# A three-stage kernel on one core: tiles of the expert items padded to one residue modulo 512 bytes, small products in fewer groups, and a reordered first item

## The chip, the cores and the metric

The kernel runs on one core of one Trainium2 chip. The metric is the device time of one execution in microseconds (us), as the median of several runs. Times inside an execution come from the profile of one execution; they count from its first instruction. Engines: PE is TensorE (PEld its weight loads), DVE is VectorE, ACT is ScalarE, POOL is GpSimd, SP is SyncE, which issues nearly all DMAs here.

## The reference

Three stages follow one another: an attention between 512 tokens and 32 states per head and batch, a mixture of 8 experts with top-1 routing and a skip, and a dense feed-forward layer.

```python
# attention: x (8,8,512,64), state (8,8,32,64) -> (8,8,544,64), both directions of a softmax
# regrouped to 4352 tokens of 512
skip_score = x @ w_skip                  # only tokens with a score over 0 are computed
logits = xc @ w_gate; e = argmax(logits) # expert of each token, gate = its softmax probability
h = np.maximum(xc[mask] @ w1[e], 0.0)    # 512 -> 1024
y[mask] = gate_w[mask, None] * (h @ w2[e])
out[do_compute] = xc + y
# dense layer, 512 -> 2048 -> 512
h = x @ w_in
g = h * np.clip(h + 3.0, 0.0, 6.0) / 6.0
return g @ w_out
```

## The kernel before

The order of the work on every engine is the order in which the program issues it; each engine runs its own queue in that order, and so does SP with the DMAs.

The attention routes each token and scatters its row to a buffer `xs` in HBM, sorted by expert. The expert stage (class `Experts`) then works through items. A large item is 512 rows of one expert: `run` does the first in `first()` and four more in `item_a(i, conv)`, i = 1 to 4. A large item has eight slices f of the hidden width. `s1a(f)` makes 12 products of 128x128 by 128x512 from `w1p` and `xTa` (L849), then a Relu on ACT (L853) and a remainder on DVE (L854) into `hT`; `s2a(po, f)` makes 12 products from `hT` and `w2p` (L861). The program issues `s1a(f)`, then `s2a(po, f - 1)`. Each operand is kept as a rounded part and a remainder, so a fetched weight slice is cut by `split1`, `split2` (ACT L761, DVE L762) before use. `end_a` ends an item: it turns the next item's rows (`turn`, L768: four transposes and a split) between the last products, gates the result on DVE (L891) and scatters it to `x_in` by four indirect DMAs on POOL (L725).

A small item is 64 rows of one expert, in plain float32 (`item_b`, a generator). In a large item i the program steps through small item i - 1: ten steps, one at f = 0 and nine at the places in `SMALL_AT`, where entry 2f is behind `s1a(f)` and 2f + 1 behind `s2a(f - 1)`. Four steps are first-layer products (L1053, 4 records each), one turns the hidden rows (L1003), four are second-layer products (L1069, 8 records each). Its weights come as eight chunks of 512 KB through three rooms; a chunk's room is refilled by SP (L1026) when the products that read it are done. Further small items, if there are any, run in a loop (`For_i`, L1112) behind the last large item.

Beside the items the kernel converts the dense layer's weights (`convert`, a generator `conv` stepped in `item_a`; fetched by `W.load`, L1219 and L1223; DVE steps L1240 to L1262) and stores them. In `first()` the list `some(n)` works through the last batch's routing (`rest`: L428, L408, L414, then counts L342, the plan of the items, the scatters) and one converted slice, stored by SP at L1306 and L1307. The second half of the plan, `second()`, is called as `k["tables"]`: three PE transposes (L652), then four DVE operations (L656 to L659) that fill `lim`, `tab_b` and `nb`.

SP's fetches for item 1 in `first()` start at f = 3: first the 512 rows (`fetchx`, L715, 1028 KB), then weight slices in pairs (`fetch1` L704, `fetch2` L710, 512 KB each), at f = 6 the small item's rows (L1016 to L1018) and three chunks (L1026).

The tiles lie one after another in each partition. The pool `a_x` holds, in this order, `raw1` twice (8192 bytes each), three `XR` slots (8480 bytes, 16·512 + 288), three `X` slots (8224 bytes, 16·512 + 32), `srows` (4112 bytes, 8·512 + 16) and `XT` (8192). `xTa` lies in `X` slots, `hT` in an `XR` slot. Behind it come small tiles and then `w1p` and `w2p` (16384 bytes a part). The dense layer (L1440, L1460, L1542, L1594) has tiles of its own whose sizes are multiples of 512 bytes; they begin below `a_x`, where its pools are closed by then.

Of the kernel before, what the change touches and what calls it, by code (L numbers as in the profile page):

```python
# [9 lines left out]
F32 = mybir.dt.float32  # L10
# [11 lines left out]
P = 128  # L22
# [4 lines left out]
XW = DM + 2  # L27

# [22 lines left out]
def attention(tc, ctx, pools, x, state, w_skip, w_gate, x_in, xs, slot, acc, count, k, consts, fill, side, early):  # L51
# [16 lines left out]
    def load(b):  # L68
        t = xp.tile([P, 4 * XW], F32, tag="X", name="X")[:, 0:4 * DM]
# [27 lines left out]
    st = xp.tile([P, 4 * 2 * NB], F32, tag="XR", name="st")[:, 0:2 * B * D].rearrange("p (g d) -> p g d", d=D)  # L97
# [294 lines left out]
    srows = xp.tile([P, 2, XW], F32, name="srows", bufs=1)  # L392
# [137 lines left out]
    def rest(plan):  # L530
# [9 lines left out]
        yield lambda: r2(b)  # L540
        pt = turned()
# [9 lines left out]
        yield lambda: r6(b)  # L551
# [38 lines left out]
Q = 64  # L590
ROUND = 1.5 * 2.0 ** 23


def plan(tc, sp, c, early, k):
# [50 lines left out]
    def second():  # L645

        pt = k["turned"]()
        vals = [red[:, 4:5], red[:, 1:2], red[:, 3:4]]
        lim, tb = k["lim"], k["tab_b"]

        def turn(i):
            nc.tensor.transpose(pt[:, i, :], vals[i].to_broadcast([P, P]), k["ident"])  # L652

        return [
            lambda: [turn(i) for i in range(3)],
            lambda: v.tensor_copy(lim, pt[:, 0, 0:NSMALL]),  # L656
            lambda: v.tensor_scalar(tb[:, 0, :], pt[0:1, 1, 0:NSMALL], 7.0, None, op0=ALU.min),
            lambda: v.tensor_scalar(tb[:, 1, :], pt[0:1, 2, 0:NSMALL], float(NSLOT), None, op0=ALU.min),
            lambda: v.tensor_scalar(k["nb"], eb[0:1, 8:9], float(NA), None, op0=ALU.max),  # L659
        ]  # L660
# [4 lines left out]
class Experts:  # L665
# [7 lines left out]
    def __init__(self, tc, pools, w1, w2, xs, x_in, k, W):  # L673
# [4 lines left out]
        self.tab_e = self.sp.tile([1, 2], I32, name="tab_e", bufs=1)  # L678
        self.room1 = [self.xp.tile([P, 4, DM], F32, name=f"raw1_{i}", bufs=1) for i in range(2)]
# [39 lines left out]
    def rows(self, name, tag="XR"):  # L719

        t = self.xp.tile([P, 4 * XW if tag == "X" else 4 * DM + 72], F32, tag=tag, name=name)
# [24 lines left out]
    def room(self):  # L746
        for i in range(2):
            t = self.xp.tile([P, 4 * XW], F32, tag="X", name=f"xTa{i}")
            self.xTa.append(t[:, 0:4 * DM].bitcast(F32R).rearrange("p (k c) -> p k c", k=4))

    def load2(self, i):
        t = self.xp.tile([P, 4 * DM + 72 * i], F32, tag="XR" if i else "XT", name="raw2", bufs=3 if i else 1)
# [21 lines left out]
    def run(self, ctx, c2, tail, plan, after):  # L774
# [30 lines left out]
        self.hT = self.xp.tile([P, 4 * DM + 72], F32, tag="XR", name="hT")  # L805
# [3 lines left out]
        keep_p = ctx.enter_context(tc.tile_pool(name="m_k", bufs=1))  # L809
        ca = ExitStack()  # L810
# [3 lines left out]
        xb = [keep_p.tile([P, DM // 2 + 2], F32, name=f"xb{i}") for i in range(2)]  # L814
        seen = keep_p.tile([P, 1], F32, name="seen")
        toks = keep_p.tile([P, 10], I32, name="toks")
        drops = keep_p.tile([P, 2], F32, name="drops")
        t = self.hT
        hT = [t[:, 4 * DM // 2 * i:4 * DM // 2 * (i + 1)].bitcast(F32R).rearrange("p (f c) -> p f c", f=NF) for i in range(2)]
        xTb = self.xp.tile([P, 2, XW], F32, tag="srows", name="xTb", bufs=1)  # L820
# [23 lines left out]
        def s1a(f):  # L844
            ph = p_h.tile([P, 512], F32, tag="h", name="ph")
            n = 0
            for kk in range(4):
                for a, b in PAIRS:
# [3 lines left out]
                    n += 1  # L852
            nc.scalar.activation(hp[f][0], ph, AF.Relu)  # L853
# [45 lines left out]

        def convert():  # L900

            todo = list(range(NEARLY, NFF))
            raw = {todo[0]: self.W.load(todo[0])}
            for i, f in enumerate(todo):
                parts, steps = self.W.cut(raw.pop(f))
                for n, step in enumerate(steps):
                    step()
                    if n == 4 and i + 1 < len(todo):
# [5 lines left out]
        def first():  # L914

            split1(0)
            split1(1)
            some(8)
            po = accs()
            for f in range(NF):  # L920
                split2(f)
                s1a(f)
# [3 lines left out]
                if f + 2 < NF:  # L926
                    split1(f + 2)
                if f == 3:
# [884 lines left out]
```

## Time and profile before

| | |
|---|---|
| runs | 1165.72, 1162.03, 1165.53 us; median 1165.53 us |
| profiled execution, its own time | 1166.02 us |
| its span, first to last instruction | 1164.3 us |
| mean granted TensorE clock | 0.985 |
| PE busy | 1112.9 us, 96% of the span |
| DVE, ACT, POOL busy | 72%, 41%, 10% |

The profile gives busy times per engine, the span in slices, the DMA queues, the chain of work that ended last, and groups of instructions by source line. The trace behind it answers questions on any stretch. A row of a timeline is start, duration, engine, line, operation, tiles, shapes and count; in brackets stands the idle time of the engine before it and what ended it. Neighbouring equal instructions are merged into one row, and matmuls overlap in part, so the time per matmul is read from the starts of consecutive runs.

### The profile page before, as it was taken

The page shows a single profiled execution, that of the slowest core. Times are in us where ns is not written, and L with a number is a line of the kernel's source. Part 1 is how long each engine was busy: PE and PEld are TensorE (multiplying, and loading weights), DVE is VectorE, ACT ScalarE, POOL GpSimd, SP SyncE. Part 2 cuts the span into 40 slices and gives each one's busy share as a digit, 9 for nine tenths or more (in the row PEclk, how much of TensorE's full clock was granted, in tenths as well). Part 3 has the DMA queues.
Part 4 walks back from the last instruction along what each step waited for, and adds up shares of the span by engine and source line. Part 5 has one row for each costly group of instructions (what it writes and reads, how often), then busy time and mean ns, then how long its engine had stood idle before and what let it go on. Part 6 is the DMA issues. An engine that isn't in the chain of part 4 may idle for free.

```text
span 1164.3 us, 16315 instructions
## 1 busy us (share of the span) xinstructions
PE 1112.9 (96%) x5978; PEld 920.0 (79%) x5978; DVE 834.1 (72%) x1632; ACT 482.0 (41%) x922; POOL 114.8 (10%) x170
## 2 busy tenths in 40 slices
PE   7887898999999949999999999999999999999998
PEld 4555676776766738888899998899989999899997
DVE  5978565766667736676788767786888678876776
ACT  6885342433333314545333244334333343334331
POOL 5466121020202020000000000000000000000000
PEclk9999898999999979999999999999999999999999
DMA  7985676987886677964552365425551454334432
GB/s 200 290 280 200 210 260 214 340 282 282 287 281 227 233 229 277 377 251 181 199 207 101 118 217 184 152 86 197 206 205 49 181 205 156 128 118 175 187 136 91
DMA packets 89074, 238.56 MB, mean 205 GB/s; under 512 B 13440, under 2 KB 40576, under 8 KB 83488
## 3 DMA queue, kind: packets, MB, share of 16 engines
q1 hardware_dynamic: 84480, 226.33, 55.2%
q0 software_dynamic: 4512, 11.17, 2.6%
q8 instruction: 48, 0.79, 0.3%
q14 instruction: 34, 0.28, 0.1%
HBM read 177.80 MB, written 63.22 MB: 207 GB/s over the span
## 4 chain that ended last, share of the span: by engine, by line
PE 61%; DVE 1%; ACT 0%; issue 0%; ACTq 0%
PE o L1594 28%; PE b L1542 24%; PE o L1460 4%; PE b L1440 4%; PE o L1371 1%; ACT g L1268 0%; PE b L1371 0%; DVE cv L1385 0%; DVE g L1269 0%; DVE c L1556 0%; DVE xt L1269 0%; DVE cv L1556 0%; DVE gg L1385 0%; ACT gg L1384 0%; DVE wc L1269 0%
## 5 line engine op out<-in xcount | busy, mean ns | idle before, releaser
L1594 PE MATMUL o<-wo,g 128*128 128x512 f32 x1440 | 334.3, 390 | 0.0
L1594 PEld LDWEIGHTS o<-wo,g 128*128 128x128 f32 x1440 | 269.7, 188 | 54.7
L1542 PE MATMUL b<-xc,wc 128*128 128x384 f32 x1680 | 299.6, 335 | 1.6 <-ACT c L1566 1.6
L1542 PEld LDWEIGHTS b<-xc,wc 128*128 128x128 f32 x1680 | 292.2, 188 | 4.0 <-ACT c L1566 1.9
L1269 DVE TENSOR_TENSOR g<-cv,g 128x384 fp32r<-128x384 f32 x160 | 89.4, 558 | 92.8 <-ACT g L1268 92.8
L1268 ACT CAST g<-cv 128x384 fp32r<-128x384 f32 x160 | 82.2, 514 | 156.9 <-DVE cv L1385 156.9
L861 PE MATMUL po<-w2p,hT 128*128 128x512 f32 x480 | 124.2, 407 | 2.3 <-ACT hT L853 2.3
L849 PE MATMUL ph<-xTa,w1p 128*128 128x512 f32 x480 | 122.8, 407 | 0.0
L861 PEld LDWEIGHTS po<-w2p,hT 128*128 128x128 f32 x480 | 90.3, 192 | 31.0 <-ACT hT L853 6.7
L849 PEld LDWEIGHTS ph<-xTa,w1p 128*128 128x128 f32 x480 | 89.8, 191 | 29.6 <-issue 9.6
L1384 ACT ACTIVATE cv<-cv,three 128x384 f32<-128x384 f32 x80 | 49.2, 615 | 143.5 <-DVE cv L1556 136.0
L1556 DVE TENSOR_TENSOR c<-b,c 128x384 f32<-128x384 f32 x160 | 87.3, 552 | 16.7 <-PE b L1542 16.2
L1603 DVE SCALAR_TENSOR_TENSOR hl<-o,hl 128x512 f32<-128x512 f32 x140 | 92.8, 683 | 2.1 <-PE o L1594 2.0
L854 DVE SCALAR_TENSOR_TENSOR hT<-ph,hT 128x512 fp32r<-128x512 f32 x40 | 27.6, 690 | 51.0 <-ACT hT L853 48.7
L853 ACT ACTIVATE hT<-ph 128x512 fp32r<-128x512 f32 x40 | 23.9, 596 | 82.5 <-PE ph L849 76.6
L1384 ACT ACTIVATE cv<-c,three 128x384 f32<-128x384 f32 x80 | 49.2, 615 | 15.0 <-DVE g L1269 15.0
L1556 DVE TENSOR_TENSOR cv<-b,cv 128x384 f32<-128x384 f32 x80 | 44.4, 555 | 14.2 <-PE b L1542 12.8
L1385 DVE SCALAR_TENSOR_TENSOR cv<-cv,c 128x384 f32<-128x384 f32 x80 | 44.2, 552 | 5.8 <-ACT cv L1384 4.8
L279 PE MATMUL pxr<-BD,AT 128*128 128x265 f32 x128 | 40.3, 435 | 8.0 <-ACT XR L283 3.4
L1603 DVE SCALAR_TENSOR_TENSOR acc<-o,acc 128x512 f32<-128x512 f32 x70 | 44.9, 683 | 1.3 <-PE o L1594 1.3
L1385 DVE SCALAR_TENSOR_TENSOR cv<-cv,cv 128x384 f32<-128x384 f32 x80 | 44.0, 550 | 0.0
L1250 ACT ACTIVATE raw<-raw 128x512 f32<-128x512 f32 x32 | 22.0, 689 | 51.5 <-DVE cv L1246 48.8
(287 smaller groups left out, 1270.1 us busy)
## 6 DMA issues: line engine op xcount, KB each, us to landing
wc<-wc SPq DMA_DIRECT2D x36, 1792.0 KB
wo<-wo SPq DMA_DIRECT2D x37, 1024.0 KB
raw<-in_moe_w_dram SPq DMA_DIRECT2D x40, 512.0 KB
spare<-in_moe_w_dram SPq DMA_DIRECT2D x32, 512.0 KB
raw<-in_moe_w_in_dram SPq DMA_DIRECT2D x16, 512.0 KB
raw<-in_moe_w_out_dram SPq DMA_DIRECT2D x16, 512.0 KB
x_in_dram<-XR SPq DMA_DIRECT2D x8, 1024.0 KB
wo<-hl SPq DMA_DIRECT2D x16, 512.0 KB
```

Of the source, the lines that this page charges most:

```text
L849: nc.tensor.matmul(ph, lhsT=w1p[a][:, f, kk, :], rhs=xTa[b][:, kk, :], start=(n == 0), stop=(n == 11))
L861: nc.tensor.matmul(po[c], lhsT=hp[f][a][:, P * c:P * c + P], rhs=w2p[b][:, f, :], start=(f == 0 and n == 0), stop=(f == NF - 1 and n == 2),)
L1268: nc.scalar.copy(hi, src)
L1269: nc.vector.tensor_tensor(lo, src, hi.bitcast(F32), op=ALU.subtract)
L1384: nc.scalar.activation(gg, h, AF.Relu, bias=k["three"])
L1385: nc.vector.scalar_tensor_tensor(gg, gg, 6.0, h, op0=ALU.min, op1=ALU.mult)
L1440: nc.tensor.matmul(ph, lhsT=w1(f, a, kk), rhs=xt[b][:, kk, :], start=(n == 0), stop=(n == 11))
L1460: nc.tensor.matmul(pos[c], lhsT=gg[a][:, P * c:P * c + P], rhs=w2(f, b), start=(f == 0 and n == 0), stop=(f == NFF - 1 and n == 2),)
L1542: nc.tensor.matmul(t, lhsT=w[:, s:s + P], rhs=XC[m // NP][:, x, b, kk, :], start=(i == 0), stop=(i == 5))
L1556: v.tensor_tensor(c, t, u, op=ALU.add)
L1594: nc.tensor.matmul(po, lhsT=gs[f][a][:, o:o + P], rhs=w[:, DM * (2 * f + b):DM * (2 * f + b) + DM], start=(q == 0), stop=(q == 5),)
L1603: nc.vector.scalar_tensor_tensor(dst, po, 1.0 / 6.0, dst, op0=ALU.mult, op1=ALU.add)
```

## The change

- Sizes. All `X` and `XR` slots become `ROWS` = 4·(512 + 32) floats, 8704 bytes, 17·512. `srows` becomes 4608 bytes. A pad of 72 floats is put ahead of `raw1`, one of 80 floats ahead of `w1p`.
- Small products. `SMALL_AT` puts them in four groups instead of eight in items 1 to 3. In item 4 (`SMALL_LAST`) the four first-layer products are in two groups and the four second-layer products come behind `end_a`; its chunks have more rooms.
- First item. `product(f + 1)` is issued ahead of `relu(f)`, `product(0)` ahead of the routing's rest; `split1(f + 2)` moves ahead of `relu`. SP fetches weights first and the 512 rows at f = 5, the chunks ahead of the small item's rows, and the first slice for `conv` at f = 7. `r6` moves ahead of the counts. `tables` is cut: one transpose and `lim` behind `end_a`, the rest in item 1 at f = 4; the load of `nb` into the engines' registers moves to item 4. `convert` fetches its next slice at its step 0 instead of 4.

```diff
+ROWS = 4 * (DM + 32)
-        t = xp.tile([P, 4 * XW], F32, tag="X", name="X")[:, 0:4 * DM]
+        t = xp.tile([P, ROWS], F32, tag="X", name="X")[:, 0:4 * DM]
-            XR[b] = xp.tile([P, 4, 2 * NB], F32, tag="XR", name="XR")
+            XR[b] = xp.tile([P, 4, ROWS // 4], F32, tag="XR", name="XR")[:, :, 0:2 * NB]
+        self.xp.tile([P, 72], F32, name="pad", bufs=1)
         self.room1 = [self.xp.tile([P, 4, DM], F32, name=f"raw1_{i}", bufs=1) for i in range(2)]
-        self.hT = self.xp.tile([P, 4 * DM + 72], F32, tag="XR", name="hT")
+        self.hT = self.xp.tile([P, ROWS], F32, tag="XR", name="hT")
+        keep_p.tile([P, PAD], F32, name="pad2")
         def first():
             split1(0)
+            ph = product(0)
             split1(1)
-            some(8)
+            split2(0)
+            some(9)
             po = accs()
             for f in range(NF):
-                split2(f)
-                s1a(f)
+                if f:
+                    split2(f)
+                now = ph
+                if f + 1 < NF:
+                    ph = product(f + 1)
+                if f + 2 < NF:
+                    split1(f + 2)
+                relu(f, now)
                 some((16, 16, 12, 10, 8, 10, 16, 12)[f])
-                if f + 2 < NF:
-                    split1(f + 2)
                 if f == 3:
-                    self.fetchx(row_a(0), xn[1])
-                    for g in range(0, 6, 2):
-                        self.fetch1(e0, g)
-                    for g in range(0, 4, 2):
-                        self.fetch2(e0, g)
+                    self.fetch1(e0, 0)
+                    self.fetch1(e0, 2)
+                    self.fetch2(e0, 0)
+                    self.fetch1(e0, 4)
+                    self.fetch2(e0, 2)
                 if f == 5:
                     self.fetch1(e0, 6)
                 if f in (5, 7):
                     self.fetch2(e0, f - 1)
+                if f == 5:
+                    self.fetchx(row_a(0), xn[1])
                 if f == 6:
-                    fetch_b(row_b(0), xb[0])
                     b0 = expert_b(0)
                     for c in range(3):
                         fetch_w(b0, c, chunks[c])
+                    fetch_b(row_b(0), xb[0])
+                if f == 7:
+                    next(conv)
             some(999)
-            for step in k["tables"]():
-                step()
             end_a(po, 0, False)
             split1(6)
             split1(7)
+            for step in tables()[:2]:
+                step()
         def item_a(i, conv):
-            small = item_b(i - 1, chunks, h32, xb[0], x32[0], hs, yb[0], 0, 1 if more else 0)
+            small = item_b(i - 1, chunks if more else chunks + free1 + chunks[:1], h32, xb[0], x32[0], hs, yb[0], 0, 1 if more else 0)
+                if f == 4 and i == 1:
+                    for step in tables()[2:]:
+                        step()
             end_a(po, i, not more)
+            for _ in small:
+                pass
-SMALL_AT = (2, 4, 5, 7, 9, 11, 12, 13, 14)
+SMALL_AT = (3, 3, 6, 6, 8, 10, 10, 14, 14)
+SMALL_LAST = (3, 3, 6, 6, 8)
```

## Rows read from the trace of the kernel before

**Rows 1.** The page's chain that ended last, shares of the span by engine.
```profile
PE 61%; DVE 1%; ACT 0%; issue 0%; ACTq 0%
```

**Rows 2.** Busy time by stage: start:end, length, engines (count), clock, DMA share, GB/s.
```profile
172.84:184.76 11.92, 9.56 (x46) 7.77 (x45) 6.54 (x15) 4.90 (x9) 0.19 (x1) 0.86 0.90 310
184.76:246.07 61.31, 58.79 (x265) 41.41 (x264) 38.04 (x66) 22.11 (x40) 6.83 (x10) 0.97 0.77 272
246.07:303.41 57.34, 57.08 (x265) 40.38 (x264) 37.51 (x65) 22.21 (x40) 7.48 (x10) 1.00 0.81 283
360.75:415.92 55.17, 55.17 (x247) 38.49 (x245) 42.13 (x72) 20.66 (x37) 8.83 (x13) 1.00 0.65 220
415.92:430.12 14.20, 0.00 (x1) 0.03 (x1) 4.75 (x10) 1.04 (x1) 3.60 (x5) 0.62 0.62 213
430.12:1164.30 734.18, 727.33 (x3640) 648.87 (x3640) 541.04 (x1009) 280.84 (x516) 0.00 (x0) 1.00 0.48 176
```

**Rows 3.** Timeline of PE in the first large item.
```profile
147.64 2.97 PE L849 MATMUL ph<-xTa,w1p 128*128 128x512 f32 x12
150.44 2.96 PE L861 MATMUL po<-w2p,hT 128*128 128x512 f32 x12
```

**Rows 4.** The chain of work in the dense layer: start, duration, what.
```profile
446.61 2.72 PE b L1440 x12
449.33 2.72 PE o L1460 x12
```

**Rows 5.** Timeline of PE in large item 2.
```profile
252.88 3.06 PE L861 MATMUL po<-w2p,hT 128*128 128x512 f32 x12
255.78 2.95 PE L849 MATMUL ph<-xTa,w1p 128*128 128x512 f32 x12
258.66 1.08 PE L1053 MATMUL phb<-spare,xTb 128*64 128x512 f32 x4
259.67 2.60 PE L861 MATMUL po<-w2p,hT 128*128 128x512 f32 x10
```

**Rows 6.** Waits of PE, 120 to 445 us: total, times, longest.
```profile
PE prl L414 <- issue: 3.0, 1, 3.0
PE ptx L768 <- DVE toks L869: 2.4, 1, 2.4
PE po L861 <- ACT hT L853: 2.3, 1, 2.3
```

**Rows 7.** Busy time of two short stretches, columns as in rows 2.
```profile
129.30:136.10 6.80, 6.62 (x21) 5.13 (x22) 2.37 (x11) 0.88 (x3) 0.75 (x2) 0.50 0.50 172
201.00:204.40 3.40, 3.40 (x9) 2.49 (x9) 2.80 (x6) 1.24 (x3) 0.00 (x0) 0.50 0.64 212
```

**Rows 8.** Timeline of DVE at the start of the first large item.
```profile
126.40 1.29 DVE L762 TENSOR_TENSOR w1p<-raw,w1p 128x512 fp32r<-128x512 f32 x2 [0.57 <-issue]
```

**Rows 9.** Timeline of PE at the start of the first large item.
```profile
130.79 5.46 PE L849 MATMUL ph<-xTa,w1p 128*128 128x512 f32 x12
```

**Rows 10.** Timeline of SP in the first large item.
```profile
158.36 0.35 SPq L715 DMA_DIRECT2D xr<-xs_dram  x1
...
164.99 1.26 SPq L710 DMA_DIRECT2D raw<-in_moe_w_dram  x1
```

**Rows 11.** Busy time of 159 to 173 us, columns as in rows 2.
```profile
159.00:173.00 14.00, 14.00 (x62) 11.21 (x62) 5.59 (x9) 4.81 (x9) 0.00 (x0) 1.00 1.02 347
```

**Rows 12.** Timeline of DVE in item 1.
```profile
197.76 0.43 DVE L1240 TENSOR_SCALAR cv<-raw 128x512 int32<-128x512 int32 x1 [8.58 <-DMA raw<-in_moe_w_out_dram]
```

**Rows 13.** Timelines of POOL, SP and DVE behind the last large item.
```profile
411.77 1.01 POOL L1081 DMA_INDIRECT x_in_dram<-xTb,toks  x1 [0.52 <-issue]
418.88 1.03 POOL L725 DMA_INDIRECT x_in_dram<-xn,toks  x1 [0.16 <-issue]
422.17 1.74 SPq L1213 DMA_DIRECT2D raw<-x_in_dram  x4
420.59 1.23 DVE L1269 TENSOR_TENSOR wc<-raw,wc 128x1024 fp32r<-128x1024 f32 x1 [1.11 <-ACT wc L1268]
```

More of the change, by code (lines that the diff above doesn't have):

```diff
@@ L651, in turn @@
         def turn(i):
-            nc.tensor.transpose(pt[:, i, :], vals[i].to_broadcast([P, P]), k["ident"])
+            if i < 2:
+                pt[0] = k["turned"]()
+            nc.tensor.transpose(pt[0][:, i, :], vals[i].to_broadcast([P, P]), k["ident"])
         return [
[L655 to L658, printed above, removed]
+            lambda: turn(0),
+            lambda: v.tensor_copy(lim, pt[0][:, 0, 0:NSMALL]),
+            lambda: (turn(1), turn(2)),
+            lambda: v.tensor_scalar(tb[:, 0, :], pt[0][0:1, 1, 0:NSMALL], 7.0, None, op0=ALU.min),
+            lambda: v.tensor_scalar(tb[:, 1, :], pt[0][0:1, 2, 0:NSMALL], float(NSLOT), None, op0=ALU.min),
             lambda: v.tensor_scalar(k["nb"], eb[0:1, 8:9], float(NA), None, op0=ALU.max),
@@ L809, in run @@
         keep_p = ctx.enter_context(tc.tile_pool(name="m_k", bufs=1))
+        xb = [keep_p.tile([P, DM // 2 + 2], F32, name=f"xb{i}") for i in range(2)]
+        seen = keep_p.tile([P, 1], F32, name="seen")
+        toks = keep_p.tile([P, 10], I32, name="toks")
+        drops = keep_p.tile([P, 2], F32, name="drops")
+        keep_p.tile([P, PAD], F32, name="pad2")
         ca = ExitStack()
@@ L844, in s1a, with product @@
         def s1a(f):
+            relu(f, product(f))
+        def product(f):
             ph = p_h.tile([P, 512], F32, tag="h", name="ph")
@@ L852, in s1a, with relu @@
                     n += 1
+            return ph
+        def relu(f, ph):
             nc.scalar.activation(hp[f][0], ph, AF.Relu)
@@ L907, in convert @@
                     step()
-                    if n == 4 and i + 1 < len(todo):
+                    if n == 0 and i + 1 < len(todo):
                         raw[todo[i + 1]] = self.W.load(todo[i + 1])
@@ L969, in item_a @@
             done = 0
+            at = SMALL_AT if more else SMALL_LAST
             for f in range(NF):
@@ L976, in item_a @@
                 s1a(f)
-                for _ in range(SMALL_AT.count(2 * f)):
+                for _ in range(at.count(2 * f)):
                     next(small)
@@ L985, in item_a @@
                     s2a(po, f - 1)
-                for _ in range(SMALL_AT.count(2 * f + 1)):
+                for _ in range(at.count(2 * f + 1)):
                     next(small)
@@ L1007, in run @@
         chunks = [t[:, 2 * DM * i:2 * DM * i + 2 * DM] for i in range(3)]
+        free1 = [t[:, 2 * c:2 * c + 2].rearrange("p u f -> p (u f)") for t in self.room1 for c in range(2)]
         h32 = t[:, 6 * DM:].rearrange("p (j c) -> p j c", j=4)
@@ L1029, in item_b @@
             e = expert_b(j)
-            n = len(room)
+            n = 3 if more == 0 else len(room)
             if more:
                 en, rn = expert_b(j + 1), row_b(j + 1)
-            elif more is None:
-                for c in range(n):
+            else:
+                for c in range(0 if more is None else n, len(room) - (more == 0)):
                     fetch_w(e, c, room[c])
             def loads(c):
-                if c + n < 8:
+                if more == 0:
+                    if c == 0:
+                        fetch_w(e, 7, room[7])
+                elif c + n < 8:
                     fetch_w(e, c + n, room[c % n])
@@ L1054, in item_b @@
                         ph[Q * o:Q * o + Q], lhsT=xt[:, c % 2, Q * (c // 2):Q * (c // 2) + Q],
-                        rhs=room[c % n][:, DM * o:DM * o + DM], start=(c == 0), stop=(c == 3),
+                        rhs=room[c % len(room)][:, DM * o:DM * o + DM], start=(c == 0), stop=(c == 3),
                     )
@@ L1064, in item_b @@
             for c in range(4):
-                w = room[(4 + c) % n].rearrange("p (u d) -> p u d", u=2)
+                w = room[(4 + c) % len(room)].rearrange("p (u d) -> p u d", u=2)
                 for q in range(2):
@@ L1098, in run @@
         both = []
-        free = [t[:, 2 * c:2 * c + 2].rearrange("p u f -> p (u f)") for t in self.room1 for c in range(2)]
+        free = free1
         for u in range(2):
-            free += [cb.tile([P, 2 * DM], F32, name=f"b{u}_{c}") for c in range(len(free), 8)]
+            free = free + [cb.tile([P, 2 * DM], F32, name=f"b{u}_{c}") for c in range(len(free), 8)]
             both.append([
@@ L1764, in items @@
             k["turned"] = lambda: pools[2].tile([P, 4, P], F32, tag="tr", name="ptt")
-            first, k["tables"] = plan(tc, pp3, count, ex.early, k)
+            first, second = plan(tc, pp3, count, ex.early, k)
+            k["tables"].append(second)
             return first
```

32 lines of the change are left out of this document (18 added, 14 removed).

## The prediction

> **What bounds the kernel now.** I read the shares of the chain that ended last first: PE holds 61% of it [rows 1], and the rest of the stages show why one can stay with PE. The table by stage comes next [rows 2]. The dense layer, 430.12 to 1164.30, is 734.2 us with PE busy for 727.3. In large item 2 (246.07 to 303.41) PE is busy for 57.08 of 57.34 us. Item 4 takes 55.17. So from 130 us on the kernel is as long as PE's queue, plus the places where PE waits. The list of PE's waits names three inside the expert stage, of 3.0, 2.4 and 2.3 us [rows 6]. After such a wait PE also runs at the lower of its two clocks (1.2 instead of 2.4 GHz): the granted clock is 0.50 from 129.3 to 136.1 and again from 201.0 to 204.4 [rows 7]. The wait between the last item and the dense layer is 14.20 us without any product [rows 2].
>
> The change can then save time in four ways: shorter products, fewer changes between the two kinds of products, fewer waits with their slow clock, an earlier end of the last item. All sums are against the profiled execution, 1166.02 us of device time with a span of 1164.3; its own time is 0.5 us above the median of the runs, 1165.53.
>
> **Padding.** In the first large item a run of 12 products starts every 2.80 us (147.64 to 150.44), 233.3 ns a product [rows 3]. In the dense layer products of the same shape and type start every 2.72 us per 12, 226.7 ns [rows 4]. What differs is where the operands lie. From the sizes: `xTa` lies in slots of 16·512 + 32 bytes, `hT` in slots of 16·512 + 288, and `w1p` behind odd small tiles, so stationary and moving operands start at different residues modulo 512; the dense layer's tiles are all multiples of 512 and share one. After the change every slot is a multiple of 512. The 288 bytes ahead of `raw1` set one residue, and the small tiles ahead of `w1p` (1056 + 1056 + 32 + 64 + 32 bytes in steps of 32) with the 320 of the second pad are 2560, 5·512, so `w1p` keeps that residue. I take the dense layer's step: 192 products by 6.6 ns, 1.27 us in each large item. The bounds are 0 (residue has no effect) and 1.27; I take 1.27, since shape, type and neighbours are those of the dense layer.
>
> On this the Trainium skill speaks against the change. "SBUF — State Buffer", section "SBUF: two separate sides", says that on the engine side only the port pair that DVE and GpSimd share causes contention, and that PE never waits on anyone. By that sentence the two operand streams of PE can't disturb each other, and the term would be 0; the rows of the two stages differ by 3%, which it leaves without a cause.
>
> **Fewer groups of small products.** A run of 12 that follows a small group takes 2.90 (252.88 to 255.78), one that stands between nothing takes 2.80, one ahead of a small group 2.88 (255.78 to 258.66) [rows 3, 5]. So a group costs 0.18 us beside its own 1.01 (258.66 to 259.67). What of the 1.01 is a fixed part no row shows: bounds 0 and 0.1 (half of what the large runs lose); I take 0.02, a cost of 0.2 us. Items 1 to 3 lose four groups each, 0.8 us; item 4 loses five, 1.0 us. The cover: a room is refilled behind the product that read it, and the next reader comes later by three runs of 12 and the rest of its group, some 9 us, where now it is four to six runs. SP must have issued and landed 512 KB by then; no PE wait on a chunk is in the list of waits [rows 6].
>
> **The first item.** Now PE starts product 0 at 130.79 at half clock and needs 5.3 us for it [rows 9], after the wait of 3.0 us for the routing's transposes and their copies [rows 6]. The operand is there sooner: two splits of `w1p` run on DVE from 126.40 for 1.29 us, so the first ends at 127.1 [rows 8]. After the change product 0 runs from 127.1 to 129.8, the routing's small products, which wait for a copy on ACT, take until about 132.7, and product 1 ends at about 135.5. Product 2 needs the bank that `relu(0)` frees, which now follows the routing's DVE work: about 136.8 (an estimate). From there 12 runs of 2.72 are 32.6: PE is ready for the turn at 169.4 instead of 172.84 [rows 2].
>
> What is late next is the item's rows. They were fetched first, at 158.36, with the weights behind them until 166.25 [rows 10]; now seven weight fetches of 512 KB go ahead of the 1028 KB, 4.72 MB together. From 159 to 173 the DMA engines are full at 347 GB/s [rows 11], so the eight take 13.6 us plus about 2 of latency. SP reaches the first of them at about 156.5: it has one register load less ahead of it, but still follows the store of a converted slice whose last DVE step is at 154. The rows are there at about 171.5 (170 to 173). PE thus waits some 2 us in place of the 2.4 for the plan's transposes and `tab_b` (now behind the item), and its clock falls for a while as it does now. The hand-over to item 1, 11.92 us now [rows 2], has 9.56 busy; I take 8.1 from the turn to item 1's first product, which puts it at 179.7 against 184.76: gain 5.0, bounds 3.0 (rows at 173, slow clock throughout) and 7.5 (rows in time).
>
> **Item 1.** It takes 61.31, item 2 57.34 [rows 2]. The 3.97 between them are the wait of 2.3 for a Relu and the slow clock after it [rows 6, 7]: DVE stood 8.58 us for the converter's slice [rows 12], and its queue holds the item's own splits and remainders behind that step. With the fetch in `first()` at f = 7 the slice follows the rows and chunks, about 180, ahead of its first use at about 182. Added are two transposes and three small DVE operations at f = 4, 0.3 us. Gain 3.97 + 1.27 + 0.8 - 0.3 = 5.7. If the slice lands late, 4.0 of it are gone.
>
> **Items 2 and 3.** 2 x (1.27 + 0.8) = 4.1.
>
> **Item 4 and the end.** SP reads the dense layer's first rows at 422.17, when the last scatter has landed; that scatter ran on POOL from 418.88 to 419.91, 4.0 behind the last product at 415.9 [rows 2, 13]. After: the large products end at 415.9 - 1.27 - 1.0 - 4.1 (four second-layer groups) = 409.5; those groups then run until 413.7 while gating and the four large scatters go on beside them. Behind the last product of the small item come a wait and 0.5 on DVE and one scatter, whose end I put 2.7 later (the row at 411.77 ends 2.7 behind its products), 416.4 against 419.91: 3.5. The converter's first tiles use the same storage as the chunks and the DVE work on them (now until 421.82 [rows 13]) can begin only at 414.6 and ends at about 419.8, level with SP's issue; bounds 2.5 and 4.5. The rest of the 14.2, barrier and loop, stays, and so does the dense layer.
>
> The attention's tiles move too. Its products are of other kinds and no row prices a moved address for them: between -1 and +1 us (a sixth of what the padding is worth in all items); I take 0, since its stage also waits on DMAs.
>
> **Sum.** 5.0 + 5.7 + 4.1 + 3.5 = 18.3; 1166.0 - 18.3 = 1147.7. I take 1147.5 as the time.
>
> **Rivals.**
> - The padding does nothing. Against it speaks the pace of the dense layer; for it, that no row here varies the address alone. Four items lose 1.27 each, item 0 loses little since its end waits for the rows: 1153.
> - The rows of item 1 come later still, since SP meets the waits of two slices (`split1(7)`, `split2(5)`) ahead of them, and PE waits 5 us or more instead of 2. For it: the full DMA engines [rows 11]. Each us costs one; with 4 more 1152.
> - The rows are in time and the clock stays up through the hand-over: 1144.
> - Slower: a refilled chunk is late. Two refills in each of items 1 to 3 now have 9 us. From a landing 12 us behind the products on, six waits of 3 us outweigh the whole gain; at 13 us, with the clock's fall added (about 1 us each), 1178 - 1148 = 30 us are lost and the time is some 1178. Against it: none of these waits exists now [rows 6], and SP's fetches are issued as soon as the products are done.
>
> **Chances.** The forecast 0.64; the rows in time 0.10; no effect of padding 0.10; rows later 0.11; slower 0.05. The range holds the first three and part of the fourth: 1142 to 1154. A difference under 0.3% (3.5 us) can't be told from none here. Of the slower case 0.04 counts as slower and 0.01 as no change, and of the late rows 0.02 as no change (18 us of loss): faster 0.93, same 0.03, slower 0.04.
>
> **What would show it.** Right: runs of 12 in the items start every 2.72; PE's product 0 starts near 127 and no clock of 0.5 follows 129; no DVE wait for the converter's slice in item 1; items 2 and 3 near 55.3; the last scatter is the small item's and SP reads `x_in` about 3.5 earlier relative to item 4's start, beside what item 4 saves before. A wait of PE of about 2 us for `xr` near 170. Wrong: runs of 2.80 as before; PE waits on L1026's chunks; a wait of over 4 us ahead of the turn; a dense layer of another length than 734.2.

## The result, and the profile after

The changed kernel takes 1148.13 us (median of 4 runs, 1147.38 to 1149.55) against 1165.62 for the kernel before beside it: a ratio of 0.9855, interval 0.9828 to 0.9881. The profiled execution took 1147.38 us with a span of 1145.7, 18.6 less than that of before; 1147.5 was forecast. The sum came out right. Its terms did so less well, and one of them, the first item's, rested on a standstill that an execution with the old order needn't have.

| stage (us) | before | after | gain | forecast |
|---|---|---|---|---|
| up to item 1's first product | 184.76 | 178.03 | 6.7 | 5.0 |
| item 1 | 61.31 | 54.95 | 6.4 | 5.7 |
| items 2 and 3 | 114.67 | 109.59 | 5.1 | 4.1 |
| item 4's start to SP's read of the dense layer's rows | 61.42 | 59.40 | 2.0 | 3.5 |
| that read to the dense layer's first product | 7.95 | 7.39 | 0.6 | 0 |
| dense layer | 734.18 | 736.30 | -2.1 | 0 |

Busy time by stage after, columns as in [rows 2]: hand-over to item 1, item 1, item 2, item 4, the gap, the dense layer, and the two stretches at half clock that answer [rows 7].

```profile
170.42:178.03 7.61, 7.61 (x43) 6.42 (x44) 5.13 (x10) 3.29 (x6) 0.20 (x1) 1.00 1.05 356
178.03:232.98 54.95, 54.95 (x268) 41.16 (x266) 38.45 (x70) 22.14 (x40) 7.85 (x10) 1.00 0.87 310
232.98:287.78 54.80, 54.72 (x265) 40.98 (x264) 37.48 (x65) 22.12 (x40) 7.38 (x10) 1.00 0.84 298
342.57:395.00 52.43, 52.40 (x247) 39.28 (x245) 42.39 (x72) 19.25 (x34) 10.53 (x15) 1.00 0.69 241
395.00:409.36 14.36, 0.03 (x3) 0.03 (x1) 4.50 (x9) 2.27 (x4) 1.70 (x2) 0.61 0.56 200
409.36:1145.60 736.24, 729.74 (x3640) 650.55 (x3640) 540.85 (x1009) 280.97 (x516) 0.00 (x0) 0.99 0.48 175
131.86:135.28 3.42, 3.42 (x10) 2.65 (x9) 3.17 (x14) 2.27 (x5) 0.13 (x1) 0.50 0.43 90
409.36:418.58 9.22, 8.54 (x27) 6.83 (x28) 2.77 (x4) 2.34 (x4) 0.00 (x0) 0.50 0.91 304
```

The items are now PE alone: item 1 is busy for all of its 54.95 us, where [rows 2] had 58.79 of 61.31. The last row is new: the dense layer's first 9.22 us run at half clock; before, the rise came 2.95 us behind its start.

PE's waits after, as in [rows 6]: the waits of 3.0, 2.4 and 2.3 are gone (0.8 is left at the place of the first); 1.5 for the rows (`xr`) and 1.0 ahead of product 0 have come.

```profile
PE o L1412 <- PEq L1852: 14.3, 1, 14.3
PE ptx L774 <- DMA xr<-xs_dram: 1.5, 1, 1.5
...
PE ph L859 <- ACT w1p L767: 1.0, 1, 1.0
PE prl L415 <- ACT sxt L410: 0.8, 1, 0.8
```

Timeline of PE in the first item (first two rows; compare [rows 3]) and in item 2 (compare [rows 5]): start, duration, what.

```profile
141.60 2.88 PE L859 MATMUL ph<-xTa,w1p 128*128 128x512 f32 x12
144.32 2.88 PE L874 MATMUL po<-w2p,hT 128*128 128x512 f32 x12
...
241.36 1.94 PE L1092 MATMUL phb<-spare,xTb 128*64 128x512 f32 x8
243.22 3.06 PE L859 MATMUL ph<-xTa,w1p 128*128 128x512 f32 x12
246.12 2.88 PE L874 MATMUL po<-w2p,hT 128*128 128x512 f32 x12
248.84 2.88 PE L859 MATMUL ph<-xTa,w1p 128*128 128x512 f32 x12
251.65 1.94 PE L1092 MATMUL phb<-spare,xTb 128*64 128x512 f32 x8
```

A run of 12 that touches no small group starts its successor 2.72 us later (246.12 to 248.84). One behind a group takes 2.90, one ahead of a group 2.81; two old groups in one take 1.86 where each took 1.01.

DVE in item 1 no longer waits for the converter's slice, compare [rows 12]; behind the last item POOL's last scatter is the small item's, and SP's read follows, compare [rows 13].

```profile
182.32 0.51 DVE L1281 TENSOR_SCALAR cv<-raw 128x512 int32<-128x512 int32 x1
```

```profile
397.22 1.01 POOL L1120 DMA_INDIRECT x_in_dram<-xTb,toks  x1 [0.15 <-issue]
...
401.97 1.74 SPq L1254 DMA_DIRECT2D raw<-x_in_dram  x4
```

The scatter ends at 398.23 and the read starts 3.74 us later; before, 2.26 lay between them.

### The profile page after: what moved, and what is told of

It reads as the page before. It is cut to its first block, busy times and chain, and to the rows that moved or that the text cites. A ratio compares the mean times of both kernels' runs of the same rounds, so it can differ in the third digit from the quotient of the medians.

```text
span 1145.7 us, 16311 instructions
## 1 busy us (share of the span) xinstructions
PE 1100.4 (96%) x5978; PEld 920.6 (80%) x5978; DVE 833.6 (73%) x1632; ACT 482.2 (42%) x922; POOL 115.7 (10%) x170
## 4 chain that ended last, share of the span: by engine, by line
PE 63%; DVE 1%; ACT 0%; issue 0%; ACTq 0%
PE o L1635 29%; PE b L1583 25%; PE o L1501 4%; PE b L1481 4%; PE o L1412 1%; ACT g L1309 0%; PE b L1412 0%; DVE cv L1426 0%; DVE g L1310 0%; DVE c L1597 0%; DVE cv L1597 0%; DVE gg L1426 0%; ACT gg L1425 0%; DVE wc L1310 0%; DVE acc L1644 0%
## 5 line engine op out<-in xcount | busy, mean ns | idle before, releaser
L859 PE MATMUL ph<-xTa,w1p 128*128 128x512 f32 x480 | 118.1, 396 | 1.1 <-ACT w1p L767 1.0
L874 PE MATMUL po<-w2p,hT 128*128 128x512 f32 x480 | 119.0, 395 | 0.0
L280 PE MATMUL pxr<-BD,AT 128*128 128x265 f32 x128 | 40.4, 436 | 8.0 <-ACT XR L284 3.6
L1607 ACT COPY c<-b 128x384 f32<-128x384 f32 x40 | 19.3, 482 | 55.1 <-PE b L1583 54.1
```

The costliest lines, as they stand in the source:

```text
L859: nc.tensor.matmul(ph, lhsT=w1p[a][:, f, kk, :], rhs=xTa[b][:, kk, :], start=(n == 0), stop=(n == 11))
L874: nc.tensor.matmul(po[c], lhsT=hp[f][a][:, P * c:P * c + P], rhs=w2p[b][:, f, :], start=(f == 0 and n == 0), stop=(f == NF - 1 and n == 2),)
```

## The experiments

They ran on three chips. On two of them the attention ends sooner (its last products start at 115.9 to 121.5 us, at 125.1 to 126.7 on the third), and the kernel before takes 1155.3 and 1155.4 us instead of 1166.4. `pad_alone`, `no_pad`, `old_groups` and `last_inside` ran on the first of these two, `w_plus128`, `conv_late`, `rows_first` and `both` on the second, the second execution of the change, `filled`, `w_plus256` and `w_plus32` on the third. So a kernel's time is set against the kernel before beside it alone, and single terms are read from the lengths of the stages, which repeat to 0.02 us in items 2 and 3. "Attention to item 1" runs from the start of the last four products of the attention (`pxr`, L279 before, L280 after) to item 1's first product; "item 4 to read" ends where SP starts to read `x_in`.

| kernel | time, ratio to before | attention to item 1 | item 1 | item 2 | item 4 to read | dense layer |
|---|---|---|---|---|---|---|
| before | | 60.44 | 61.31 | 57.34 | 61.42 | 734.18 |
| after | 1148.13, 0.9855 (0.9828 to 0.9881) | 54.62 | 54.95 | 54.80 | 59.40 | 736.30 |
| after, again | 1149.37, 0.9852 (0.9832 to 0.9871) | 54.02 | 54.95 | 54.78 | 59.07 | 735.88 |
| pad_alone | 1152.68, 0.9980 (0.9961 to 0.9998) | 54.11 | 60.71 | 56.58 | 62.35 | 734.41 |
| no_pad | 1147.26, 0.9922 (0.9895 to 0.9949) | 54.10 | 55.90 | 55.77 | 59.88 | 735.99 |
| old_groups | 1147.99, 0.9925 (0.9896 to 0.9955) | 55.32 | 56.76 | 56.57 | 59.60 | 734.25 |
| last_inside | 1143.32, 0.9898 (0.9870 to 0.9926) | 53.70 | 54.96 | 54.78 | 61.26 | 734.40 |
| conv_late | 1150.98, one run | 54.53 | 61.26 | 54.79 | 59.18 | 736.39 |
| rows_first | 1139.05, one run | 53.78 | 54.96 | 54.79 | 59.26 | 734.15 |
| both | 1140.47, 0.9872 (0.9851 to 0.9893) | 53.09 | 54.96 | 54.78 | 56.34 | 734.77 |

**Padding alone, and all but padding.** `pad_alone` is the kernel before with the new sizes; `no_pad` is the changed kernel with the old ones.

```diff
-            t = self.xp.tile([P, 4 * XW], F32, tag="X", name=f"xTa{i}")
+            t = self.xp.tile([P, ROWS], F32, tag="X", name=f"xTa{i}")
...
+        keep_p.tile([P, PAD], F32, name="pad2")
```

> The kernel before with the tile sizes of the change alone; order and groups stay the old ones. Theory (the residue of the addresses sets the products' pace): runs of 12 products in the items start every 2.72 us instead of 2.80; items 2 and 3 take 57.34 - 1.27 = 56.1 us each, item 4 from its first product to its last 55.17 - 1.27 = 53.9; with 1.3 in item 1 and up to 1 in item 0 the time falls by 5 to 6, to about 1160. Rival (the place of the operands is without effect, as the Trainium skill says in SBUF - State Buffer, section SBUF: two separate sides, where PE never waits on anyone): runs of 12 stay at 2.80, items at 57.3, the time within 1 us of 1165.6; the pace of 2.72 after the change then comes from its new order.

> The changed kernel with the old tile sizes. Theory: runs of 12 go back to 2.80 us, items 2 and 3 take 54.80 + 1.27 = 56.07, all items and item 0 together 5 to 6 us, so about 1153.5. Rival: runs stay at 2.72, items at 54.8 and the time at 1148. If padding is worth more than 1.27 an item (the two items came out 0.45 shorter than I forecast), up to 1.7 each: items at 56.5 and 1155.

Item 2 of `pad_alone`, then of `no_pad` (columns as in [rows 2]):

```profile
232.32:288.90 56.58, 56.31 (x265) 40.30 (x264) 37.62 (x65) 22.19 (x40) 7.38 (x10) 1.00 0.83 287
```

```profile
231.47:287.24 55.77, 55.69 (x266) 41.03 (x264) 37.35 (x65) 22.11 (x40) 7.48 (x10) 1.00 0.83 292
```

The addresses do set the pace: the mean spacing of two starts in a stream of the item goes from 233.6 to 229.3 ns with the old groups and from 233.6 to 228.2 with the new ones. But an item gains 0.76 with the old groups and 0.97 with the new (57.34 to 56.58, 55.77 to 54.80), not the 1.27 that I took from the dense layer. The reason shows in the spacing of single starts: in the padded kernels a stream is at 226.7 ns only from the sixth to the twelfth product behind a group or a transpose on; the ones before it, behind a first of 313 to 342, stand 223 to 240 ns apart. The steady runs of the dense layer, from which I took the pace [rows 4], have no such breaks. The Trainium skill ("SBUF — State Buffer", section "SBUF: two separate sides") says that PE never waits on anyone there. The trace doesn't agree with the term of 0 that I had read from it: nothing but addresses differs between `no_pad` and the changed kernel, and the product takes 233.6 or 228.2 ns. What PE waits for in that time no row shows.

The whole falls by 2.6 us in `pad_alone`, not by 5 to 6: item 1 gains 0.6, item 4 up to its last product 0.8, and SP's read behind it comes later, not sooner (62.35 for 61.42).

`pad_alone` also surprised in another place: with the old order of the first item it needs 54.11 us from the attention to item 1, as little as the changed kernel, where before had needed 60.44. This is taken up below.

**Which residue.** Three times only the second pad's size changes, by which `w1p` and `w2p` move 256, 32 and 128 bytes against the tiles that they are multiplied with.

```diff
-PAD = 80
+PAD = 144
```

> The changed kernel with a second pad of 144 elements instead of 80: w1p and w2p lie 256 bytes further modulo 512, all else stays. Theory (the operands of a product must be equal modulo 512): steady runs of 12 at 2.80 us, items 2 and 3 at 55.77 as without padding. Rival (a smaller period, 256 bytes or a part of it, is enough): steady runs at 2.72, items at 54.80.

> The changed kernel with a second pad of 88 elements instead of 80: w1p and w2p lie 32 bytes further, all else stays. Theory (any difference modulo 512 costs the same): runs of 2.80 us, items 2 and 3 at 55.77. Rival 1 (the cost grows with the distance): runs between 2.72 and 2.80, items at 54.9 to 55.3. Rival 2 (the old pace came from other tiles than these): 2.72 and 54.80.

> The changed kernel with a second pad of 112 elements instead of 80: w1p and w2p lie 128 bytes further modulo 512. 256 bytes further cost nothing (steady products every 227 ns, items 54.79), 32 bytes cost all (items 55.73). Theory (the operands must be equal modulo 256): runs of 2.80, items 2 and 3 at 55.75. Rival (modulo 128 or 64): 2.72 and 54.79.

PE in item 2, 256 bytes off, 32 bytes off, 128 bytes off:

```profile
241.55 2.88 PE L874 MATMUL po<-w2p,hT 128*128 128x512 f32 x12
244.36 1.94 PE L1092 MATMUL phb<-spare,xTb 128*64 128x512 f32 x8
```

```profile
241.01 2.96 PE L874 MATMUL po<-w2p,hT 128*128 128x512 f32 x12
243.90 1.94 PE L1092 MATMUL phb<-spare,xTb 128*64 128x512 f32 x8
```

```profile
237.07 2.96 PE L874 MATMUL po<-w2p,hT 128*128 128x512 f32 x12
239.97 1.94 PE L1092 MATMUL phb<-spare,xTb 128*64 128x512 f32 x8
```

From run to group: 2.81, 2.89, 2.90 us; item 2 takes 54.79, 55.72 and 55.59, the whole 1148.61, 1150.79 and 1145.91 (one run each, the last on another chip). So 256 bytes off costs nothing, 32 and 128 bytes cost nearly what the old addresses cost (55.77). The rule that the change follows, equality modulo 512, is more than is needed; of the distances tried, equality modulo 256 is enough and modulo 128 is not. In all three `xTa` and `hT` stayed where they were, and no run moved all operands together: that their equality counts, and not the place of `w1p` and `w2p` by itself, isn't shown.

**The groups.** The old list of places in items 1 to 3.

```diff
-SMALL_AT = (3, 3, 6, 6, 8, 10, 10, 14, 14)
+SMALL_AT = (2, 4, 5, 7, 9, 11, 12, 13, 14)
```

> The changed kernel with the old eight groups of small products in items 1 to 3; item 4 stays as changed. By the 0.2 us a group of the prediction: items 2 and 3 take 54.80 + 4 x 0.2 = 55.6, the time 1148.1 + 2.4 = 1150.5. Rival, that a change between the two kinds of products costs 0.3 or more: items at 56.0 to 56.2, the time about 1152. If what the items lost beyond the forecast is padding's and not the groups', it is 55.6.

Timeline of PE in item 2 of this kernel:

```profile
237.44 1.08 PE L1092 MATMUL phb<-spare,xTb 128*64 128x512 f32 x4
238.45 3.02 PE L874 MATMUL po<-w2p,hT 128*128 128x512 f32 x12
241.31 2.88 PE L859 MATMUL ph<-xTa,w1p 128*128 128x512 f32 x12
244.12 1.08 PE L1092 MATMUL phb<-spare,xTb 128*64 128x512 f32 x4
```

Item 2 takes 56.57 instead of 54.79 here, 1.78 more: 0.44 for each of the four groups, even above the rival's 0.3. Added up over the starts of all products of the item, the small products take 8.09 us instead of 7.49 (0.15 a group: the fixed part that I had set at 0.02), the runs stand 2.42 instead of 1.44 above 226.7 ns a product (0.25 a group, where I had 0.18), and the transposes take 2.53 instead of 2.35. This last part isn't a break but a wait: with the old places PE stands 0.26 us at the turn for DVE's `xTb` (L1114), with the new ones it doesn't. A group itself thus costs 0.40.

**The end of item 4.** The small item's products spread inside item 4, so that a large scatter is the last.

```diff
-SMALL_LAST = (3, 3, 6, 6, 8)
+SMALL_LAST = SMALL_AT
```

> The changed kernel with the small products of the last item spread inside it, as in items 1 to 3, so that the large scatters come last. Theory (the scatter that is issued last sets the end): the last large product is at 395.0 + about 0.5, its scatter ends 4.0 later at about 399.5 instead of 398.2, SP reads the dense layer's rows 1 to 1.5 us later than 59.40 after item 4's start, the time is about 1149.4. Rival (the transfers of the converter's last slices, which fill the DMA engines from 387 to 400, set the landing, whichever scatter is last): the read stays at 59.4 +- 0.4 behind item 4's start and the time at 1148.1.

Item 4 to the read takes 61.26 instead of 59.07 to 59.40, some 2 us more: the place of the last group is worth what the theory said and more, and the rival falls in that form. But the last scatter ends at 390.70 and the read comes at 395.37, 4.67 behind it:

```profile
389.69 1.01 POOL L731 DMA_INDIRECT x_in_dram<-xn,toks  x1 [0.16 <-issue]
```

```profile
395.37 1.74 SPq L1254 DMA_DIRECT2D raw<-x_in_dram  x4
```

So the scatter's end isn't the whole of it: here, as after the change (3.74), it lands late. So it does in `pad_alone`, which has the old end of item 4 (404.28 to 407.81, 3.53): the 2.26 of before is the exception.

**The converter's first fetch.**

```diff
-            yield
...
-                if f == 7:
-                    next(conv)
```

> The changed kernel with the converter's first slice fetched in item 1, as before, and not behind the last products of the first item. Theory (of item 1's gain of 6.4 us 4.0 come from this fetch): DVE waits some 8 us for the slice in item 1, PE 2.3 us for a Relu and then runs at half clock for a while; item 1 takes 54.95 + 4 = 59. Rival (the slice is late, but the new order leaves DVE enough ahead): item 1 at 55 to 56.

Busy time of item 1 and of a stretch in it; then DVE and PE there:

```profile
174.69:235.95 61.26, 57.77 (x267) 42.74 (x266) 38.38 (x70) 22.00 (x40) 7.13 (x10) 0.94 0.81 278
190.01:196.83 6.82, 5.35 (x13) 4.07 (x14) 5.70 (x10) 4.29 (x9) 0.00 (x0) 0.50 0.61 194
```

```profile
188.57 0.43 DVE L1278 TENSOR_SCALAR cv<-raw 128x512 int32<-128x512 int32 x1 [9.51 <-DMA raw<-in_moe_w_out_dram]
```

```profile
191.48 2.07 PE L874 MATMUL po<-w2p,hT 128*128 128x512 f32 x4 [3.49 <-ACT hT L866]
```

The chain is the one foretold: DVE stands 9.51 us for the slice, PE 3.49 for the Relu behind it, then half clock. Its price is not: item 1 loses 6.3 us, not 4.0, and is as long as before the change (61.31). Without the fetch the slice's landing sets item 1's end, and what padding and groups save is waited away: PE's wait is 3.5 instead of 2.3 and the half clock lasts 6.8 us instead of 3.4.

**The order of rows and weights.**

```diff
                     e0 = expert_a(0)
+                    self.fetchx(row_a(0), xn[1])
...
-                if f == 5:
-                    self.fetchx(row_a(0), xn[1])
```

> The changed kernel with the rows of item 1 fetched ahead of its weights again. Theory (the rows were 1.4 us late for the turn, and the weights have time): no wait of PE for the rows, product 0 to item 1 takes 51.9 - 1.4 = 50.5, item 1 stays at 54.95. Rival (the weights, 3 us later, are late for the splits of f = 5 to 7, behind which the remainders of the products stand in DVE's queue): PE waits for DVE or ACT near the end of the first item, and it takes 52 to 54.

PE's waits in this kernel, and its wait at the turn:

```profile
PE ptx L774 <- DVE xTa L768: 1.3, 2, 0.8
PE ph L859 <- ACT w1p L767: 1.0, 1, 1.0
```

```profile
166.42 0.66 PE L774 MATMUL ptx<-ident,xr 128*128 128x128 f32 x4 [0.81 <-DVE xTa L768]
```

PE doesn't wait for the rows, yet attention to item 1 takes 53.78, only 0.24 to 0.84 less than the two executions of the changed kernel, and product 0 to item 1 51.69 instead of 50.5: of the 1.4 that I expected, 0.81 is lost to a wait on DVE's splits of the turned rows (the other 0.5 of the 1.3 lies in the attention, as after the change). The first of the two, with 0.84, is the fairer comparison: there, as here, product 1 ran at half clock (126.11 to 129.53 here), in the second it didn't. No weights are late: item 1 takes 54.96. Rows first is worth some 0.8 us here.

**The clock at the dense layer's start.** The changed kernel again, and with 54 products behind the last small one.

```diff
+        ph = p_h.tile([P, 512], F32, tag="h", name="fill")
+        for n in range(54):
+            nc.tensor.matmul(ph, lhsT=w2p[0][:, 0, 0:P], rhs=w2p[0][:, 1, :], start=(n == 0), stop=(n == 53))
         self.W.early()
```

> The changed kernel once more, to have its stages from a second execution, on the same chip as the next three. Theory (items and hand-overs are fixed by their instructions, while the time of the attention ahead of them and the phase of the clock at the dense layer's start vary from execution to execution): item 1 54.95, items 2 and 3 54.80, item 4 to SP's read 59.4, each +- 0.1; product 0 starts anywhere from 117 to 131 us; the dense layer takes 734.2 to 736.3, longer the longer its start lies in half clock (734.2 with 2.95 us of it before the change, 736.3 with 9.22 after). Rival: the 2.1 us that the dense layer lost belong to the change, and it takes 736.3 again.

> The changed kernel with 54 more products of 128x512 (their sum is read by nobody) behind the last small product, 12.2 us, so that PE has work until some 2 us ahead of the dense layer. Theory (the half clock at the dense layer's start comes from the 14 us without products): no clock of 0.5 there, the dense layer starts as late as before, about 67 us behind item 4's start, and takes about 733.2 (by 0.34 us for each us of half clock, from 736.30 with 9.22 us and 734.18 with 2.95). Rival 1: the clock falls in the remaining 2 us all the same and it takes 734 to 736. Rival 2: the products are still running when the other engines meet, and the dense layer starts later by what they overlap.

The changed kernel's second execution, its stretch of half clock in the dense layer; then PE and the stretch of half clock with the filling products:

```profile
411.80:420.07 8.27, 7.59 (x25) 6.08 (x26) 2.77 (x4) 2.34 (x4) 0.00 (x0) 0.50 0.86 290
```

```profile
397.26 12.53 PE L1136 MATMUL fill<-w2p 128*128 128x512 f32 x54
411.71 3.15 PE L1415 MATMUL o<-ident,raw 128*128 128x128 f32 x16 [1.92 <-PEq L1855]
```

```profile
412.25:419.07 6.82, 6.14 (x21) 4.72 (x20) 2.76 (x4) 2.35 (x4) 0.00 (x0) 0.50 0.88 276
```

Filling the gap didn't save the clock: it was up when the dense layer began, fell 0.5 us later and stayed down for 6.82 us. The layer took 735.15, and the ratio of this kernel to before (0.9849) can't be told from that of the change (0.9852). The theory's 733.2 fell, rival 1 held. Without the filling the rise comes 2.8 to 9.2 us behind the layer's start, and the layer's length follows it: 734.15 with 2.83 (`rows_first`), 734.18 with 2.95 (before), 734.50 with 4.29 (`w_plus256`), 735.88 with 8.27, 736.30 with 9.22, 736.39 with 9.24 (`conv_late`); `both`, 734.77 with 3.49, lies a little off this row. Kernels with the same end as the change, `w_plus256` and `rows_first`, had the short ones, so the 2.1 us needn't belong to the change. But of the ten executions with its end four had a rise 8 to 9 us behind the start, both of the change itself among them, and of the three with the old end none: that it makes them likelier isn't excluded. The second execution repeats the items to 0.02 us; its read, 59.07, came 0.33 sooner than the first's, more than the 0.1 foretold.

**A version with two more edits.**

```diff
                     self.fetch1(e0, 4)
+                    self.fetchx(row_a(0), xn[1])
                     self.fetch2(e0, 2)
...
-                if f == 5:
-                    self.fetchx(row_a(0), xn[1])
...
-CONVERTED = (3, 3, 3, 5)
+CONVERTED = (3, 3, 4, 4)
...
-                while done < steps * (f + 1) // (NF - 1) and done < steps:
+                while done < steps * (f + 1) // (NF - 1 - (not more)) and done < steps:
```

> The changed kernel with two edits in places that the changed kernel left waiting. (1) The rows of item 1 go ahead of two of the five first fetches of weights: they land some 3 us sooner, PE doesn't wait for them, product 0 to item 1 takes 50.5 instead of 51.9. Rival: weights are late instead, 52 or more. (2) One slice of the converter moves from item 4 to item 3 and item 4's are done by f = 5: their stores and re-reads leave the DMA engines some 7 us sooner. Theory (the scatters' landing was late since those transfers filled the engines until 400): SP's read of the dense layer's rows comes 58.0 us behind item 4's start instead of 59.4. Rival (a scatter needs 3.7 us to land anyway): 59.4 again; and item 3, with 9 more steps on DVE, may pass 54.8. By the theories the time is 2.8 us below the changed kernel's, a ratio of 0.983 to the kernel before.

SP in item 4 and behind it, POOL's last scatter, and busy time of the stretch around it in this kernel; then the same stretch of the changed kernel:

```profile
376.55 0.32 SPq L1346 DMA_DIRECT2D wo<-hl  x1
...
395.44 1.74 SPq L1253 DMA_DIRECT2D raw<-x_in_dram  x4
```

```profile
392.89 1.01 POOL L1119 DMA_INDIRECT x_in_dram<-xTb,toks  x1 [0.15 <-issue]
```

```profile
391.60:393.90 2.30, 0.00 (x0) 0.00 (x0) 2.20 (x6) 0.98 (x3) 1.69 (x2) 1.00 0.33 121
```

```profile
396.00:398.23 2.23, 0.00 (x0) 0.00 (x0) 2.13 (x6) 0.90 (x3) 1.70 (x2) 0.97 1.02 399
398.23:400.00 1.77, 0.00 (x0) 0.00 (x0) 0.88 (x3) 0.82 (x1) 0.00 (x1) 0.50 0.83 313
400.00:401.97 1.97, 0.00 (x0) 0.00 (x0) 1.23 (x1) 0.23 (x1) 0.00 (x0) 0.50 0.05 19
```

This bears out the theory of the landing. The converter's last stores start 37.5 us behind item 4's start instead of 43.7, the DMA engines are 0.33 busy around the last scatter instead of full (after the change they are full until about 400, and the last packets, at 19 GB/s, take until the read), and the read follows the scatter's end by 1.54 us instead of 3.74. Item 4 to the read is 56.34. But item 3 pays back 1.93 of the 2.7 to 3.1 us gained: it takes 56.72, with new waits of PE of 1.1 us for a chunk of the small expert and of 0.4 for its rows:

```profile
PE phb L1091 <- DMA spare<-in_moe_w_dram: 1.1, 1, 1.1
...
PE ptx L1037 <- DMA xb<-xs_dram: 0.4, 1, 0.4
```

The first item takes 51.0 from product 0, 0.9 less than in the changed kernel's second execution, which like this one has no half clock there (0.5 short of what was expected, for a wait of 0.8 on DVE's splits, as in `rows_first`). Items 3 and 4 together give 0.8 to 1.1, so that by stages this version is a little under 2 us better than the change. Its ratio to before, 0.9872 (0.9851 to 0.9893), was taken on another chip than the change's and doesn't show that; that it beats the change is open.

## Why the prediction was right

**The sum** (18.3 for 18.6) was right by luck, since errors of both signs cancelled: the early terms gave 3.4 more than forecast, the last item 1.5 and the dense layer 2.1 less, the way between them 0.6 more.

**The first item (6.7 for 5.0): the size lay within the bounds, the cause is settled in part.** Of the 6.7 us, 0.9 are an earlier end of the attention. The remaining 5.8 I had put down to the new order: product 0 ahead of the routing's products, no half clock behind the wait. But `pad_alone`, with the old order, needs 54.11 from the attention to item 1, and `no_pad`, with the new order, 54.10; before needed 60.44. What before had and `pad_alone` lacked is a standstill of ACT ahead of the copy that the routing waits for. First before, then `pad_alone`:

```profile
128.95 0.48 ACT L409 COPY sxt<-pts 128x384 f32<-128x384 f32 x1 [2.12 <-remote]
```

```profile
119.91 0.48 ACT L410 COPY sxt<-pts 128x384 f32<-128x384 f32 x1
```

ACT stood for 2.12 us for something that the profile calls remote; PE's wait was 3.0 [rows 6] instead of 0.8, and product 0 ran at half clock [rows 9]. I took that wait for the order's work, and it is at least in part an event of that execution or that chip.

Against `pad_alone` the new order takes as much as it gives. From the attention's last products to the turn `pad_alone` needs 42.5 us, the second execution of the change 46.4: it has new waits of PE of 1.0 ahead of product 0, 0.8 for a remainder ahead of product 2 and 1.4 for the rows. From the turn to item 1 `pad_alone` needs 11.58, with the old wait of 2.4 and half clock, the change 7.61:

```profile
160.03:171.61 11.58, 9.21 (x44) 7.47 (x43) 6.50 (x15) 4.79 (x9) 0.19 (x1) 0.85 0.96 327
```

`no_pad`, on the same chip as `pad_alone`, has 46.0 and 8.06. Before had 48.8 and 11.60, so that of the 5.8 us 4.0 come from the hand-over, which takes 7.6 to 8.6 in every execution with the new order, and 1.8 from ahead of the turn, where before lost 6.3 us more than `pad_alone` (some 1.1 of it by the pace of its 14 unpadded runs, an estimate). Without such a loss the new order is no gain there. That the new order covers such a standstill (ACT now waits out product 0 at that place) is argued, not shown. It also bears on the total: by the stages, `no_pad`, `old_groups` and `last_inside` cost 3.4, 5.6 to 6.3 and 1.9 us against the change, which puts the change at 1141 to 1144 on their chip (an estimate), 11 to 14 below before there, not 17. The ratio of 0.9852 on the third chip, where before takes 1166.4, speaks for the chip and not for a single execution. Before's trace from the faster chips, which would settle it, is missing.

The steps inside: product 0 started at 125.50, not 127.1 (0.9 of it the attention's); product 1 did run at half clock (131.86 to 135.28), against the forecast that no 0.5 would follow 129, yet product 2 came at 136.07, near the 136.8. PE was ready for the turn at 169.0 (169.4) and waited 1.46 us for the rows (some 2). They were there at 170.4, 15.8 us behind SP's first fetch at 154.61; the forecast's own terms, 156.5 + 13.6 + 2, add up to 172.1 and not to the 171.5 that it states. The clock didn't fall behind that wait, against what I had expected: hence 7.6 us from the turn to item 1 instead of 8.1. So padding brings little in this item: without it PE waits 0.4 us for the rows (`no_pad`), with it 1.4 to 1.5 (the change's two executions).

**Item 1** (6.4 for 5.7): the term was right, but not as a sum of parts. All of it hangs on the one fetch, 6.3 by `conv_late`; I had put 4.0 on it.

**Items 2 and 3** (5.1 for 4.1): both parts were mis-sized in opposite ways. Padding, 1.27 in the forecast, is 0.97 with the new groups and 0.76 with the old, as the pace of unbroken streams was laid on broken ones. Four groups, 0.8 in the forecast, are 1.6 without and 1.8 with padding. The step that failed most is the bound on the fixed part of a group, 0 to 0.1 with 0.02 taken: it is 0.15. The part beside a group is 0.25 for 0.18, and the wait on `xTb` makes up the rest. Rows of two lengths of group would have shown it; all groups of before have the same length.

**Item 4** (2.0 for 3.5): the last scatter ended 55.66 us behind the item's start instead of 59.16, exactly the 3.5 foretold. I had then carried over the 2.26 us from there to the read; after the change it was 3.74, as the scatter fell into the converter's transfers. `both` shows it by moving these. With the old end of item 4 the landing can be as late (`pad_alone`, 3.53), and against that execution the new end is worth 2.95 (62.35 to 59.40).

**The dense layer** (-2.1 for 0): the forecast named another length than 734.2 as a sign of error, but had no term for the phase in which the clock rises, worth up to 2.2 us.

**The rivals.** That padding does nothing falls (`no_pad`). Rows still later didn't come. The slower case, late chunks, didn't come either, but its mechanism exists: one more slice in item 3 is enough for a chunk 1.1 us late (`both`).

## What to carry to other kernels

Measure the cost of leaving a stream of products from its break, both sides and inside, and not from the steady runs; going from eight groups to four was worth more here (1.6 to 1.8 us an item) than aligning every operand (0.8 to 1.0). Where a stage ends by a transfer, saved engine time is waited away until that transfer is issued sooner, and a term for it isn't added to the others but decides whether they count. Before putting a wait down to the order of the work, see whether a second execution has it.

## What the hardware showed beyond that

The pace of fp32r products of 128x512 depends on where their operands lie: 226.7 ns in an unbroken stream with stationary and moving operand equal modulo 256 bytes, about 233 ns when they are 32 or 128 bytes off; 128 bytes off the starts alternate between 229 and 237 ns in some runs of 12. Behind a group of other products or a transpose the first product takes 313 to 342 ns and four to ten more stand 223 to 240 ns apart; the last one ahead of a group takes about 318. This pattern repeats within 2 ns from item to item and from execution to execution. A clock that is up at the start of the dense layer can still fall half a microsecond into it, behind 1.9 us without work and short transposes.
